# A long convolution by Fourier transform: 128 x 32 with 64x64 tiles becomes 256 x 16 with 32x32 tiles, under a new order

## The chip, the cores and the metric

The kernel runs on one core of a Trainium2 chip. The core has engines that work side by side, each through its own list of instructions in order: TensorE for matrix products (PE in the profile, with its weight loads shown apart as PEld), VectorE (DVE), ScalarE (ACT), GpSimd (POOL) and SyncE (SP). POOL and SP do little but start DMA transfers here. Matrix products land in PSUM, which has eight banks of 128 partitions by 512 float32 numbers; from there an engine must copy ("evict") them to SBUF, the working memory. The metric is the device time of one execution in microseconds (us), lower is better.

## What is computed

Two independent heads work on 2048 positions of 1024 channels, and their outputs stand side by side in the result.

```python
# head A: short convolution, product, long convolution, gate
k_shift = sum(k_pad[:, t:t + S, :] * shift_k[:, ks - 1 - t] for t in range(ks))   # ks = 4
kv = k_shift * v
y = irfft(rfft(pad(kv)) * rfft(pad(ssm_k)))[:S]          # causal, length 2048 of 4096, per channel
a = q * (y + kv * ssm_D)

# head B: a diagonal complex state space model
Lam_bar = exp(dt * Lam);  B_bar = ((Lam_bar - 1) / Lam)[:, None] * (B_re + 1j * B_im)
h[t] = Lam_bar * h[t - 1] + B_bar @ x[t]                 # 1024 states, 2048 steps
b = 2 * real((C_re + 1j * C_im) @ h[t]) + x[t] * Dskip
```

## The kernel before

**Head B** goes in 16 chunks of 128 positions. For chunk i, 8 tasks `U` (16 matmuls of 128 columns each, L444) make the input projection; `ue` evicts it (ACT); `r1`, `r2`, two scans `sc`, `r3`, `r4` on DVE (L459 to L478) turn it into the states, one after the other from chunk to chunk; eight tasks `y.i.dh.part` (L518, L521), each of four 512-column matmuls and one of 128 columns, make the output products; `ye` evicts and `yst` stores. For chunks 6 to 12 the output products are instead written as `yt` (L499) in 64x64 tiles: the array is used as four small ones, and each matmul has 64 rows and 64 columns of weights. Their skip products are then `yk` (L484). `yf` or a drain guards the first accumulation.

**Head A** is a Fourier transform of 4096 points in three steps, by matrix products with constant matrices. Positions are split as 16 residues `s` by 128.

- *First stage.* `kvm`, `kva`, `kvb`, `kvc` (DVE) make kv for one residue; `am` (L573) multiplies it with F1, two matmuls per half of the channels; `ae` (ACT) evicts, `ast` (POOL) writes it to Ys_kv in DRAM. The filter is transposed (`hT`, `hc`), multiplied by the same matrix (`hm`, L611), evicted (`he`) and written to Ys_h (`hst`). F1 holds zeros in every other row of each of its two halves, one half per parity.
- *Middle stage.* It works on 16 pairs i. `lw` loads the pair's constants into one of three weight slots (`wslot`), `lh` and `lk` load 256 rows of Ys_h and Ys_kv. `sh` and `sk` (L640) transform the filter and kv, `she` and `ske` evict. `sw` copies the filter's real and imaginary rows crosswise by DMA, `pr` (DVE, L666) multiplies, `sa` (L678) transforms back, `sae` evicts, `vst` writes to Vs in DRAM. One `sh`, `sk` or `sa` does half a pair: 4, 4 and 8 matmuls of 64x64 weights by 512 columns, into two PSUM banks.
- *Last stage.* `vl` reads Vs, `a3` (L706) multiplies by G, `a3e` evicts, `qm` gates by q (`qp` loads it), `ost` stores.

All of Ys_h must be in DRAM before the first `lh` can load, all of Ys_kv before the first `lk`, all of Vs before the first `vl`.

**The order** is written out by hand as one long string, `ORDER`. Each word is a task; it issues its instructions at once, so each engine's list, the DMA lists of SP and POOL included, is the string's order cut down to that engine. Behind a colon stand the places that the task uses: `a` for places in one big SBUF arena, `p` for the PSUM banks, `w` for weight slots, `h` for the three state buffers. Nothing else sets priorities: an engine that waits for one task holds up all that follow on it.

Of the kernel before, what the change touches and what calls it, by code (L numbers as in the profile page):

```python
# [21 lines left out]
N1, N2, NFFT = 128, 32, 4096  # L22
NG = 32
NPAIR = NG // 2
NUNITS = 53
NGS = 3
NWS = 3
# [5 lines left out]
def a_constants():  # L33
    g = np.arange(NG)[:, None, None]; l = np.arange(2)[None, :, None]; cc = np.arange(2)[None, None, :]
    k1 = (2 * g + l + 0 * cc).reshape(-1); cs = (cc + 0 * g + 0 * l).reshape(-1)
    m = np.arange(128)
    ang = 2 * np.pi * (m // 2)[:, None] * (k1 + 0.5)[None, :] / N1
    tr = np.where(cs[None, :] == 0, np.cos(ang), -np.sin(ang))
    F1 = np.stack([tr * (m % 2 == p)[:, None] for p in range(2)], axis=1)
    G = np.stack([tr.T * (m % 2 == p)[None, :] * 2 / NFFT for p in range(2)], axis=1)  # L40
    n2 = np.arange(N2); k2 = np.arange(N2)
    W = np.zeros((2, 64, NG, WC))
    for g in range(NG):
        for l in range(2):
            kk = (2 * g + l) + N1 * k2
            phi = 2 * np.pi * np.outer(n2, kk + 0.5) / NFFT
            cph, sph = np.cos(phi), np.sin(phi)
            fw = np.zeros((2, N2, 2, N2))
            fw[0, :, 0, :] = cph
            fw[1, :, 0, :] = sph  # L50
            fw[0, :, 1, :] = -sph
            fw[1, :, 1, :] = cph
# [11 lines left out]
    return f(F1), f(G), f(W)
# [5 lines left out]
wb.3:p4 par_rest tabA2 wbe.3 gz bT.1.1:p5 kp.-1 x.1:a29 U.1.0.0:a30p6 wbe.5 kp.0 wbe.7 kvm.1:a32 kva.1 bT.1.0:p7 kvb.1:a28 bc.1.1 bc.1.0 bl.6.0:a36  # L70
bl.7.1:a37 bl.3.1:a38 bl.7.0:a39 bT.6.1:p0 bc.6.1 bT.6.0:p4 bT.7.1:p1 bc.6.0 bc.7.1 kp.1 kvm.3:a40 kvm.2:a44 kva.3 U.1.0.1 bT.7.0:p3 bT.3.1:p5 bc.7.0
sin1 bc.3.1 U.1.3.0:p7 U.1.3.1 sin2 eo x.0:a48 ue.1.0 U.0.0.0:a50p0 U.0.0.1 U.0.3.0:p4 U.0.3.1 bl.4.1:a49 bc.2.0 ue.0.3 bT.4.1:p1 bc.4.1 ue.0.0 kp.-2
kvm.0:a0 x.2:a52 U.2.0.0:a8p3 kvb.3:a49 U.2.0.1 U.2.3.0:p5 U.2.3.1 ue.2.3 kva.0 bl.3.0:a10 x.5:a11 bl.2.1:a36 bT.2.1:p6 bc.2.1 U.5.0.0:a38p2
U.5.3.0:p4 bl.5.1:a37 bT.5.1:p1 bc.5.1 U.5.3.1 ue.5.3 stt cx.5.0 bl.4.0:a32 z1 bT.3.0:p0 bT.4.0:p5 x.3:a33 kp.2 bc.3.0 bl.5.0:a34 U.1.1.0:p6 kvb.0:a35
U.0.1.0:p1 kvm.4:a40 kva.2 bc.4.0 kva.4 cx.6.1 vp.0:a36 kvc.1 cl.1.1:a10 kvb.4:a32 bT.5.0:p4 cl.2.0:a0 bc.5.0 kvb.2:a1 U.0.1.1 ue.0.1 U.0.2.0:p0
U.0.2.1 ue.1.3 cl.3.1:a2 cl.2.1:a3 cx.7.0 ue.0.2 r1.0:a40 kvc.0 ue.2.0 r2.0:h0 kvm.5:a44 rt sc.0.0 lw.3:w0 sc.0.1 U.1.2.0:p5 U.1.1.1 ue.1.1 U.1.2.1
cl.1.0:a34 ue.1.2 U.5.0.1 ue.5.0 z2 r1.1:a40 r3.0:a20 cT.3.1:p4 U.5.1.0:p1 U.5.1.1 cT.2.0:p7 dd r2.1:h1 ue.5.1 U.3.0.0:a50p0 cx.5.1 cx.6.0 U.3.2.0:p3
U.3.3.0:p6 cl.3.0:a2 cT.1.1:p5 r4.0 U.3.3.1 cc.1.1 ue.3.3 kva.5 cc.3.1 U.3.2.1 cT.2.1:p2 cc.2.1 ue.3.2 U.2.2.0:p1 U.3.0.1 cT.1.0:p5 cc.1.0 cl.0.1:a0
cT.0.1:p6 cc.0.1 am.0.0:p4p2 ae.0.1.0:a36 ue.3.0 ae.0.0.0 U.2.1.0:p3 U.2.1.1 ue.2.1 cT.3.0:p5 cc.2.0 cy.1 am.0.1:p6p2 sc.1.1 ae.0.0.1 ae.0.1.1 sc.1.0
cx.4.0 cl.0.0:a10 U.2.2.1 ue.2.2 r1.2:a24 r3.1:a40 am.1.0:p0p4 r4.1 cx.7.1 U.5.2.0:p3 am.1.1:p7p6 vp.1:a30 cx.4.1 U.5.2.1 ue.5.2 kvc.2 cc.3.0  # L80
# [87 lines left out]
def full_kernel(ctx, tc, A_q, A_k, A_v, A_shift_k, A_ssm_k, A_ssm_D, B_x, B_Lre, B_Lim, B_Bre, B_Bim,  # L168
# [613 lines left out]
```

## Time and profile before

| | |
|---|---|
| median of 3 runs | 358.2 us (356.83 to 359.08) |
| profiled execution | 357.8 us, span 356.1 us |
| granted TensorE clock, mean | 0.995 of full speed |
| instructions in the span | 10361 |
| DMA | 104.10 MB, mean 292 GB/s |
| evictions of the middle stage on ACT | 3 groups of 64, about 0.65 us each |
| wslot loads | 16 of 160 KB, median 3.8 us to landing |

The span runs from the first to the last instruction that the profile shows. A busy time is the union of the instructions' durations on one engine; matmuls overlap, so a group's mean duration is longer than the time between two starts. "Idle before" names what ended the wait ahead of an instruction. L12 is line 12 of the kernel.

### The profile page before, as it was taken

What the parts mean: (1) busy time and instruction counts of PE and PEld (TensorE: products, weight loads), DVE (VectorE), ACT (ScalarE), POOL (GpSimd) and SP (SyncE); (2) the same over time, 40 slices, a digit from 0 to 9 for tenths busy, and PEclk for the clock granted to TensorE, in tenths of its full rate; (3) what the DMA queues carried; (4) which work ended last, traced back from release to release, by engine and by line L of the source; (5) the groups of instructions that cost most, each with busy time, mean ns of one, the idle gap of its engine ahead of it and who ended that gap; (6) DMA issues with size and microseconds to landing.
All of it is one profiled execution on the core that took longest, in us unless ns stands there. A gap on an engine that the chain in (4) does not pass through costs nothing.

```text
span 356.1 us, 10361 instructions
## 1 busy us (share of the span) xinstructions
PE 333.2 (94%) x4378; PEld 232.8 (65%) x4393; DVE 314.1 (88%) x239; ACT 285.4 (80%) x547; POOL 87.5 (25%) x142
## 2 busy tenths in 40 slices
PE   5999999999999999999979999898989998999991
PEld 2889998465947669766835667464766875944440
DVE  4899999999999999999987997987498769997970
ACT  5899998257799989999578998888989996546550
POOL 5000000021515333436140205121421422300250
PEclk9999999999999999999999999999999999999997
DMA  6999987598999999999989999989889998899973
GB/s 212 319 262 299 234 135 202 195 298 190 297 224 353 317 326 296 276 299 322 323 278 337 327 328 352 307 298 324 312 321 308 349 345 290 330 317 389 371 284 148
DMA packets 62826, 104.10 MB, mean 292 GB/s; under 512 B 29582, under 2 KB 31646, under 8 KB 62780
## 3 DMA queue, kind: packets, MB, share of 16 engines
q1 hardware_dynamic: 50012, 59.78, 59.0%
q0 software_dynamic: 12768, 43.67, 33.6%
q8 instruction: 34, 0.56, 0.7%
q14 instruction: 12, 0.10, 0.1%
HBM read 53.62 MB, written 35.13 MB: 249 GB/s over the span
## 4 chain that ended last, share of the span: by engine, by line
PE 63%; DMA 13%; ACT 10%; issue 6%; DVE 4%; POOL 2%; SPq 1%; POOLq 0%; DVEq 0%; ACTq 0%
PE bank L444 24%; PE bank L518 13%; PE bank L499 6%; DMA wslot<-a_c_W 4%; DMA arena<-arena 4%; PE bank L573 4%; PE bank L611 4%; DMA arena<-Xs 3%; ACT BT L414 3%; PE bank L678 2%; PE bank L595 2%; PE bank L640 2%; DVE gslot L472 2%; PE bank L398 2%; DMA arena<-in_B_B_re_dram 2%
## 5 line engine op out<-in xcount | busy, mean ns | idle before, releaser
L444 PEld LDWEIGHTS <-BT 128*128 128x128 bf16 x2048 | 117.9, 98 | 11.2 <-issue 4.3
L444 PE MATMUL bank<-arena,BT 128*128 128x128 bf16 x2048 | 123.8, 220 | 1.5 <-ACT BT L414 0.8
L472 DVE TENSOR_TENSOR_SCAN gslot<-rtab,gslot 128x1040 bf16<-128x1040 f32 x32 | 72.7, 2310 | 3.9 <-ACT gslot L468 3.5
L518 PE MATMUL bank<-CT,gslot 128*128 128x512 bf16 x275 | 68.7, 379 | 0.7
L499 PE MATMUL bank<-CT,gslot 64*64 64x512 bf16 x896 | 56.3, 376 | 0.4 <-DVE gslot L478 0.4
L666 DVE TENSOR_TENSOR arena<-arena 128x4096 bf16<-128x4096 bf16 x16 | 36.6, 2290 | 17.4 <-ACT arena L656 7.6
L446 ACT CAST arena<-bank 128x512 bf16<-128x512 f32 x64 | 39.0, 641 | 10.1 <-PE bank L444 9.8
L518 PEld LDWEIGHTS <-gslot 128*128 128x128 bf16 x288 | 26.3, 98 | 27.4
L499 PEld LDWEIGHTS <-gslot 64*64 64x64 bf16 x896 | 28.6, 107 | 20.6 <-DVE gslot L478 0.9
L656 ACT CAST arena<-bank 128x512 bf16<-128x512 f32 x64 | 36.2, 658 | 5.6 <-PE bank L640 4.7
L649 ACT CAST arena<-bank 128x512 bf16<-128x512 f32 x64 | 35.0, 637 | 4.7 <-issue 1.5
L617 ACT CAST arena<-bank 128x512 bf16<-128x512 f32 x64 | 35.2, 672 | 4.1 <-PE bank L611 2.9
L686 ACT CAST arena<-bank 128x512 bf16<-128x512 f32 x64 | 35.5, 660 | 3.2 <-PE bank L678 3.0
L579 ACT CAST arena<-bank 128x512 bf16<-128x512 f32 x64 | 35.7, 629 | 2.9 <-PE bank L573 2.9
L459 DVE TENSOR_TENSOR arena<-gslot,Z 128x4096 bf16<-128x4096 bf16 x16 | 36.6, 2289 | 0.7
L459 DVE TENSOR_TENSOR arena<-arena,Z 128x4096 bf16<-128x4096 bf16 x16 | 36.5, 2282 | 0.7 <-ACT arena L446 0.6
L660 POOL DMA_DIRECT2D arena<-arena x32 | 17.4, 547 | 70.6 <-ACT arena L649 60.9
L620 POOL DMA_DIRECT2D Ys_h<-arena x32 | 23.3, 730 | 35.8 <-ACT arena L617 35.8
L640 PE MATMUL bank<-arena,wslot 64*64 64x512 bf16 x256 | 23.7, 382 | 6.8 <-DMA wslot<-a_c_W 4.1
L553 DVE TENSOR_TENSOR arena<-arena 128x4096 bf16<-128x4096 bf16 (+3 forms) x16 | 30.0, 1880 | 0.0
L527 ACT CAST arena<-bank 128x512 bf16<-128x512 f32 x32 | 19.8, 645 | 11.4 <-PE bank L521 9.9
L582 POOL DMA_DIRECT2D Ys_kv<-arena x16 | 11.1, 695 | 64.1 <-ACT arena L579 64.0
(101 smaller groups left out, 421.1 us busy)
## 6 DMA issues: line engine op xcount, KB each, us to landing
Ys_kv<-arena POOLq DMA_DIRECT2D x16, 512.0 KB, 6.5
Ys_h<-arena POOLq DMA_DIRECT2D x32, 256.0 KB, 4.7
arena<-Ys_h SPq DMA_DIRECT2D x16, 512.0 KB, 5.4
arena<-arena POOLq DMA_DIRECT2D x32, 256.0 KB, 4.6
arena<-Ys_kv SPq DMA_DIRECT2D x16, 512.0 KB, 7.7
Vs<-arena POOLq DMA_DIRECT2D x16, 512.0 KB, 6.5
arena<-Vs SPq DMA_DIRECT2D x16, 512.0 KB, 6.7
arena<-in_A_k_dram SPq DMA_DIRECT2D x8, 512.0 KB, 5.4
```

What stands on the lines that cost most here:

```text
L444: nc.tensor.matmul(pu[:, w, jl, :], BT[:, 2 * jp + jl, w, d, :], xT[:, d, :], start=(d == 0), stop=(d == ND - 1))
L446: E["ue"] = lambda i, jp: nc.scalar.copy(st["u", i][:, :, 2 * jp:2 * jp + 2, :], st.pop(("pu", i, jp)))
L459: nc.vector.tensor_mul(m, s_, win(Z))
L472: nc.vector.tensor_tensor_scan(gf, rtab[:].rearrange("p j t -> p (j t)"), gf, 0.0, ALU.mult, ALU.add)
L499: mm = nc.tensor.matmul(st["py", i, dh][64 * c:64 * c + 64, :], h[rows, w, j, 2 + 64 * c:66 + 64 * c], CT[rows, j, w, dh * 512:(dh + 1) * ...
L518: nc.tensor.matmul(py, h[:, w, j, 2:GW], CT[:, j, w, dh * 512:(dh + 1) * 512], start=(j == 0 and w == 0), stop=False)
L579: return nc.scalar.copy(st["ysb", n2][:, p, dh * 512:(dh + 1) * 512], st.pop(("pa", n2, p, dh)))
L617: return nc.scalar.copy(st["yh", hf, s][:, p, e, :], st.pop(("pb", hf, s, e, p)))
L649: return nc.scalar.copy(st["hab", i][:, 0, a, l, :], st.pop(("ps", "h", g, l)))
L656: return nc.scalar.copy(st["x16", i][:, a, l, :], st.pop(("ps", "k", g, l)))
L666: nc.vector.tensor_mul(hab, st.pop(("x16", i)).rearrange("p a l d -> p (a l d)").unsqueeze(1).to_broadcast([P, 2, 2 * D]), hab)
L686: return nc.scalar.copy(st["vsb", i][:, a, dh * 512:(dh + 1) * 512], st.pop(("pv", g, dh)))
```

## The change

The transform is factored 256 x 16 instead of 128 x 32. F1 becomes one full matrix of 128 rows by 256 outputs, used as two halves, and G likewise; the number and shape of the first-stage and last-stage matmuls stay. Rows of Ys_kv, Ys_h and Vs are numbered (half, row, residue) instead of (row, half, residue).

The middle stage has weights of 32x32 in place of 64x64. One `sh`, `sk` or `sa` now does a whole pair, with 16, 16 and 32 matmuls of 32x32 weights by 512 columns, which go to four row groups and four column groups of the array, into four banks. A pair's constants take 320 columns instead of 640, so `lw` loads 80 KB. Evictions, crosswise copies, the product `pr` and the stores keep number and size.

`yt`, `yk` and `yf` are used no more: all output products are `y` on the whole array. The last product with q and its store are made in halves for two residues (`qh`, `oh`). `ORDER` is new throughout, all places included; of it the diff shows the beginning and the lines around the first `sh`.

```diff
-N1, N2, NFFT = 128, 32, 4096
-NG = 32
-NPAIR = NG // 2
+N1, N2, NFFT = 256, 16, 4096
+NPAIR = 16
...
+    a = np.arange(128)
+    kc = np.arange(256)
+    ang = 2 * np.pi * a[:, None] * (kc // 2 + 0.5)[None, :] / N1
+    tr = np.where(kc[None, :] % 2 == 0, np.cos(ang), -np.sin(ang)).reshape(128, 2, 128)
+    G = tr.transpose(2, 1, 0) * 2 / NFFT
...
-    wslots = [const.tile([P, 2 * WC], BF16, name="wslot%d" % s) for s in range(NWS)]
+    wslots = [const.tile([P, WC], BF16, name="wslot%d" % s) for s in range(NWS)]
...
-    Yk_w = Ys_kv.rearrange("(k p s) d -> s k p d", p=2, s=16)
+    Yk_w = Ys_kv.rearrange("(p k s) d -> s k p d", p=2, s=16)
...
-    def s2(nm, g):
-        i, a = divmod(g, 2)
-        for l in range(2):
-            st["ps", nm, g, l] = bank()
-        for dh in range(2):
-            for l in range(2):
-                rows = slice(64 * l, 64 * l + 64)
-                nc.tensor.matmul(st["ps", nm, g, l][64 * dh:64 * dh + 64, :], st["w", i][rows, a * WC:a * WC + 64],
-                                 st[nm, i][rows, a, dh * 512:(dh + 1) * 512], start=True, stop=True)
+    def s2(nm, i):
+        for r in range(4):
+            st["ps", nm, i, r] = bank()
+        for g in range(2):
+            for dh in range(2):
+                o = 32 * (2 * g + dh)
+                for r in range(4):
+                    rows = slice(32 * r, 32 * r + 32)
+                    nc.tensor.matmul(st["ps", nm, i, r][o:o + 32, :], st["w", i][rows, 32 * g:32 * g + 32],
+                                     st[nm, i][rows, g, dh * 512:(dh + 1) * 512], start=True, stop=True)
...
+    def sa(i):
+        for b in range(4):
+            st["pv", i, b] = bank()
         for t in range(2):
-            for l in range(2):
-                for dh in range(2):
-                    rows = slice(64 * dh, 64 * dh + 64)
-                    c0 = a * WC + 64 + 128 * l + 64 * t
-                    nc.tensor.matmul(st["pv", g, dh][64 * l:64 * l + 64, :], st["w", i][rows, c0:c0 + 64],
-                                     st["hab", i][rows, t, a, l, :], start=(t == 0), stop=(t == 1))
+            for r in range(4):
+                c0 = 64 + 32 * (4 * t + r)
+                for b in range(4):
+                    rows = slice(32 * b, 32 * b + 32)
+                    nc.tensor.matmul(st["pv", i, b][32 * r:32 * r + 32, :], st["w", i][rows, c0:c0 + 32],
+                                     st["hab", i][rows, t, r, :], start=(t == 0), stop=(t == 1))
...
+    def qh(n2):
+        ot, qt = (st[nm, n2 // 2][:, n2 % 2, :] for nm in ("ot", "qt"))
+        nc.vector.tensor_mul(ot, ot, qt)
+    E["oh"] = lambda n2: spd(oar[:, n2, :], st["ot", n2 // 2][:, n2 % 2, :])
...
-ld_par ld_w:a0 wb.0:p0 par_T:p1 p32 wb.4:p2 wbc:a4 bl.6.1:a52 wbe.0 wb.7:p3 exp1 dve2 wbe.4 wb.6:p4 wbe.6 exp2 wb.1:p5 wbe.1 bl.1.1:a8 dve3 bl.0.1:a9
-bT.0.1:p6 bc.0.1 wb.2:p7 wbe.2 sm_pre sin0 bl.0.0:a10 bT.0.0:p0 bc.0.0 bl.1.0:a11 ld_F wb.5:p1 kring:a12 tabA1:a20a22a24a26 bl.2.0:a28 bT.2.0:p2
...
-hst.1.1.1 hst.1.5.0 hst.1.2.1 hst.1.6.1 hst.1.2.0 hst.1.5.1 hst.1.7.1 hst.1.7.0 lh.1:a26 sh.2:p1p0 she.2.0:a0 she.2.1 sh.3:p7p5 she.3.0 ast.12
-yt.6.0.2 yt.6.0.3 she.3.1 lh.0:a30 sh.0:p3p4 she.0.1:a20 she.0.0 yk.7.0:p1 yk.7.1:p0 sh.1:p7p5 yf.6.she.0.1 yt.6.1.0 ast.15 she.1.0 she.1.1 ast.14
-ast.13 lh.3:a48 sh.6:p4p3 she.6.0:a4 yt.6.1.1 she.6.1 sh.7:p7p5 lh.2:a40 yt.6.1.2 she.7.1 lk.1:a10 sk.3:p4p3 she.7.0 ske.3.0:a48 yt.6.1.3 sk.2:p5p7
...
+bT.0.0:p2 sm_pre wb.3:p1 bl.7.0:a16 tabA1:a18a20a22a24 exp2 wbe.5 wbe.0 bl.6.1:a17 sin0 par_rest wbe.6 bc.0.0 wbe.2 wbe.3 bT.7.0:p6 kp.0 kp.-2 tabA2
+kp.1 kp.-1 kvm.1:a28 kvm.3:a32 kvm.0:a36 kva.3 kvm.2:a40 kvb.3:a52 kva.2 kva.1 bT.6.1:p7 bc.6.1 bc.7.0 bl.0.1:a26 kva.0 kvb.2:a27 kvb.0:a16 kvb.1:a17
...
+sc.8.0 sc.8.1 hst.1.4.0 r3.8:a24 hst.1.4.1 hst.1.0.1 y.6.0.2 y.6.0.3 r4.8 hst.1.3.0 y.7.0.0:p3 hst.1.5.1 qp.5:a36 xl.14:a12 hst.1.2.0 hst.1.5.0
+hst.1.2.1 xs.15 hst.1.3.1 hst.1.1.0 hst.1.1.1 xl.12:a13 hst.1.6.1 ue.9.1 xl.10:a14 hst.1.6.0 lh.1:a42 sh.1:p2p0p6p5 she.1.1:a4 she.1.0 she.1.2 y.7.0.1
+she.1.3 lh.3:a50 sh.3:p7p1p0p2 she.3.1:a32 y.7.0.2 y.7.0.3 she.3.2 she.3.0 y.7.1.0:p6 y.7.1.1 y.7.1.2 she.3.3 ast.11 lh.0:a2 sh.0:p5p1p0p7 she.0.0:a16
+she.0.1 she.0.2 she.0.3 y.7.1.3 ast.13 ye.7.1:a15 y.8.1.0:p2 ast.10 y.8.1.1 ast.14 ast.15 ast.12 sw.1.0 lh.2:a10 ye.7.0 lk.1:a44 ye.6.0 sk.1:p5p1p0p7
```

More of the change, by code (lines that the diff above doesn't have):

```diff
@@ L33, in a_constants @@
 def a_constants():
[L34 to L40, printed above, removed]
@@ L63, in a_constants @@
     f = lambda a: np.ascontiguousarray(a.reshape(128, -1), dtype=np.float32).astype(ml_dtypes.bfloat16)
[L64 removed]
+    return f(tr), f(G), f(W)
 ORDER = """
[L68 to L70 removed]
@@ L71 @@
[L71 to L78, printed above, removed]
@@ L165 @@
+ost.6 y.15.1.1 y.15.0.3 y.15.1.2 oh.14 y.15.1.3 a3e.3.1 a3e.3.0 qm.1 ye.15.0:a13 ye.15.1 ost.1 yst.15
 """
@@ L211, in full_kernel @@
     W3v = W3d.ap().rearrange("p (i m) -> p i m", i=NPAIR)
-    Ys_kv = tc.dram_tile([NG * P, D], BF16, name="Ys_kv")
-    Ys_h = tc.dram_tile([NG * P, D], BF16, name="Ys_h")
-    Vs = tc.dram_tile([NG * P, D], BF16, name="Vs")
+    Ys_kv = tc.dram_tile([NFFT, D], BF16, name="Ys_kv")
+    Ys_h = tc.dram_tile([NFFT, D], BF16, name="Ys_h")
+    Vs = tc.dram_tile([NFFT, D], BF16, name="Vs")
     Xs = [tc.dram_tile([P, D], BF16, name="Xs%d" % i) for i in range(NCH)]
```

252 lines of the change are left out of this document (125 added, 127 removed).

## The prediction

> **What bounds the kernel now.** I first read the page's busy times, then the busy time of each engine by stage. Stage A runs to the first middle matmul (L640) at 175.3 us, stage B to the last one (L678) at 302.9, stage C to the end. The columns are stage, length, then busy time and instruction count of PE, PEld, DVE, ACT and POOL.
>
> ```profile
> PE 333.2 (94%) x4378; PEld 232.8 (65%) x4393; DVE 314.1 (88%) x239; ACT 285.4 (80%) x547; POOL 87.5 (25%) x142
> 175.30:302.90 127.60, 118.68 (x2065) 78.90 (x2066) 106.53 (x54) 112.09 (x228) 31.87 (x53) 1.00 0.92 322
> 302.90:356.10 53.20, 45.29 (x348) 25.80 (x344) 38.96 (x24) 25.10 (x51) 10.35 (x16) 0.97 0.84 306
> 14.20:175.30 161.10, 159.67 (x1918) 122.26 (x1928) 160.05 (x133) 138.26 (x255) 40.25 (x59) 1.00 0.98 269
> ```
>
> In A, PE and DVE are both full from 14.2 us on. In C, PE alone is full until its last matmul. In B, PE, ACT and DVE are all over 80% and none is full.
>
> Busy PE is not PE at work, since matmuls overlap; so I take slots from start to start, out of the order of time (start, length).
>
> ```profile
> 171.80 3.74 PE L444 MATMUL bank<-arena,BT 128*128 128x128 bf16 x64
> 175.46 1.91 PE L499 MATMUL bank<-CT,gslot 64*64 64x512 bf16 x29
> ...
> 224.97 0.39 PE L640 MATMUL bank<-arena,wslot 64*64 64x512 bf16 x4
> 225.19 1.03 PE L499 MATMUL bank<-CT,gslot 64*64 64x512 bf16 x16
> 226.05 0.39 PE L640 MATMUL bank<-arena,wslot 64*64 64x512 bf16 x4
> ...
> 225.84 0.12 PEld L640 LDWEIGHTS <-wslot 64*64 64x64 bf16 x4
> ...
> 302.28 1.03 PE L499 MATMUL bank<-CT,gslot 64*64 64x512 bf16 x16
> 303.25 0.95 PE L444 MATMUL bank<-arena,BT 128*128 128x128 bf16 x14
> ```
>
> Sixteen 64x64 matmuls take 0.86 us (225.19 to 226.05): four share the array, and a group of four costs 0.216, as much as one full matmul of 512 columns. Inside a group the starts lie close together: four weight loads of 107 ns fill 0.12 us, so some 4 ns apart. A full matmul of 128 columns costs 0.056. Entering the tiled form costs 0.09 (64 at 0.056 are 3.58; the next starts after 3.66), leaving it 0.10 (four groups are 0.86; the next starts after 0.97). So 0.195 for a visit.
>
> With these slots I add up the orders. B holds 38 U (34.0), 53 yt (45.8), 12 yk (2.7), 128 middle groups (27.6) and 15 visits (2.9): 113.1 of 127.6 us. PE loses 14.5 there, mostly to waits:
>
> ```profile
> PE bank L640 <- DMA wslot<-a_c_W: 4.1, 4, 1.7
> PE bank L640 <- DMA arena<-Ys_kv: 2.7, 2, 2.3
> PE bank L678 <- DVE arena L666: 1.1, 1, 1.1
> ```
>
> C has 45.7 us of PE work and ends its matmuls 45.7 us after it began; a tail of 7.4 follows (last eviction and store).
>
> **The change, part by part.**
>
> *Middle stage.* 512 matmuls of 64x64 in 128 groups become 1024 of 32x32 in 64 groups of sixteen. No row shows a 32x32 group. If sixteen run side by side, it costs 0.216 and the stage 13.8 instead of 27.6; if only four do, 0.86 and 55.3. I take 0.216: the 64x64 rows show full overlap with different data in each column half, and sixteen starts at 3.5 ns are 0.056, well inside 0.216. The low bound below that is excluded, as 512 columns pass in any case.
>
> *Output products.* yt (64x64 tiles) goes; every y runs on the whole array. A chunk costs the same: 32 slots of 0.216 against 128 quarter slots. But before, yt lay next to the middle tasks in one tiled form. Now each middle task stands between whole-array work: reading the new order gives 44 visits, not 15. A visit costs 0.195 plus the wider spread of sixteen starts (0.042): 0.237, so 10.4 us instead of 2.9.
>
> Over the whole kernel PE goes from 323.5 + 2.9 to 309.6 + 10.4: 6.4 us less, not 13.8.
>
> [...] In this trace loads for the same rows run under matmuls (PEld L499 is loading from 224.98 us, under L640) and the period stays 0.216. [...]
>
> *New order, stage A.* Before the first `sh`, the new order has 57 y instead of 48 y, 2 yt and 2 yk: PE +6.1. DVE has more. The last output product ahead of `sh.1` is y.7.0.0, which waits for r4.7; before it was yt.6, waiting for r4.6:
>
> ```profile
> 173.26 1.22 DVE L478 TENSOR_TENSOR gslot<-arena 128x2048 bf16<-128x2048 bf16 x1
> ```
>
> That is r4.6, done at 174.5, just ahead of the first tiled matmul. All kv work lies ahead of it in both orders, so r4.7 comes one chunk later: r1, r2, two scans, r3, r4 at mean 2.29, 1.22, 2.31, 2.31, 2.29, 1.22, less some 0.08 overlap each, 11.2 us. DVE is full, so nothing hides it: r4.7 at 185.7, and after one y part (0.92) the first `sh` at 186.6. PE's own sum would allow 3 us earlier, which also covers four k loads (2 MB) that SP now issues ahead of most B loads. Should they hold up kvm.1 beyond 14.2 us, every microsecond is lost whole.
>
> *Stage B.* 40 U (35.8), 44 y (40.5), 64 groups (13.8), 44 visits (10.4): 100.5. Of the 14.5 lost I keep 11.8. The wait for Ys_kv (2.7) goes: between first `sh` and first `sk` PE has nine y parts (8.3) and three groups, against 5 yt and six groups before. The wslot waits stay: loads halve to 80 KB, but most reloads have 3.0 to 3.3 us of PE work over them where 3.3 to 3.9 stood. A 160 KB load took 3.8 to land, 64 KB 3.0, so the half load saves 0.6 or so, and the cover is 0.5 thinner. B takes 112.3, to 298.9.
>
> *Stage C.* 45.8 of PE work; behind the last `sa` stand 8 U and 11 y (17.3) for the V round trip, which took 12.9 before (302.9 to the first V landed at 315.8). With the tail, 53.2: the span is 352.1.
>
> *At nothing:* F1t, Gt and stage-three matmuls keep number and shape; Ys and Vs rows are renumbered with pieces of the same size; evictions stay 64 each; the two halves qh cost DVE 0.15 more at the end, where it idles.
>
> **Sum.** 352.1 + 1.7 (execution 357.8 against its span of 356.1) = 353.8. The median, 358.2, is 0.4 over that execution. I say 354.
>
> **Rivals.**
>
> *Evictions set stage B.* ACT's evictions follow each other at 0.48:
>
> ```profile
> 225.40 0.58 ACT L656 CAST arena<-bank 128x512 bf16<-128x512 f32 x1
> 225.89 0.59 ACT L686 CAST arena<-bank 128x512 bf16<-128x512 f32 x1
> 226.36 1.58 ACT L656 CAST arena<-bank 128x512 bf16<-128x512 f32 x3
> ```
>
> B keeps 188 middle evictions, 20 ue and 11 ye: 219 x 0.477 = 104.5, now above PE's 100.5. If ACT is kept as full as PE was (113.1 of 127.6, 89%), B takes 118 and the time is 186.6 + 118 + 53.2 + 1.7 = 359.5. For it: ACT is 88% busy in B now. Against: its in-order queue idled mostly for PE. [...]
>
> *Four banks at once (slower).* A middle task held two banks and now holds four of eight; its first four matmuls touch all of them. Freeing four takes 4 x 0.477 = 1.9 us, and PE, in order, stops with everything behind it when one is late. 48 tasks times a wait w: from w = 0.17 us on it is slower by over 1%; at 0.4, 373. For it: y parts hold one or two banks for several parts. Against: none of PE's waits listed in B is for ACT, so banks have come free in time so far.
>
> *Sixteen tiles do not overlap.* At four side by side, 41.5 us more on PE in B: about 395. Against it stand the 64x64 rows.
>
> **How the numbers follow.** My forecast has a chance of 0.47 (346.5 to 357: the low end is ACT's floor of 104.5 in B; 0.41 of it faster by over 1%, 0.06 within). Evictions: 0.27 (356 to 363; 0.24 within, 0.03 slower). Banks: 0.20 (0.02 within, 0.18 slower). No overlap: 0.06, slower. One per cent, about what a measurement of this kernel can tell from no change, is 354.6 to 361.8. Faster 0.41, same 0.32, slower 0.27. The range, 346.5 to 368, leaves out the no-overlap case and the worse half of the bank case.
>
> **What would show it.** Right: sixteen 32x32 starts within 0.06 us and the next group after 0.216; 44 visits at 0.24; first `sh` near 186.6; B near 112 and C near 53. Wrong: `sh` waiting on ACT for banks; ACT full through B; groups longer than 0.3; or a first `sh` that is earlier because DVE ran ahead.

## The result, and the profile after

The changed kernel takes 370.4 us (median; 369.2 to 370.8) where the kernel before, beside it on the same chip, takes 357.9: a ratio of 1.034, 95% interval 1.030 to 1.039. It is slower, and above the top of the forecast range. Some executions of every kernel are disturbed and take 1 to 3% longer; the ratios here and below leave them out, the medians do not.

From the page of the changed kernel, the row of the granted clock in 40 slices of 9.2 us:

```profile
PEclk9999999999999999999996999998999999999997
```

Busy time of each engine by stage (start and end, length, busy time and instruction count of PE, PEld, DVE, ACT, POOL, then granted clock, DMA share, GB/s), first of the kernel before, then of the changed kernel:

```profile
0.00:177.22 177.22, 171.10 (x2008) 129.11 (x2022) 170.43 (x164) 149.13 (x271) 45.23 (x73) 1.00 0.97 268
177.22:302.07 124.85, 115.93 (x2018) 77.40 (x2013) 103.88 (x53) 110.79 (x225) 31.87 (x53) 1.00 0.92 320
302.07:356.05 53.98, 46.12 (x364) 26.26 (x360) 39.79 (x24) 25.51 (x51) 10.35 (x16) 0.97 0.84 308
```

```profile
0.00:192.47 192.47, 177.16 (x2009) 131.86 (x2023) 183.83 (x172) 150.37 (x273) 46.80 (x75) 1.00 0.91 249
192.47:315.33 122.86, 107.73 (x1870) 66.49 (x1884) 88.76 (x45) 109.08 (x224) 30.56 (x51) 0.96 0.89 317
315.33:369.00 53.67, 45.89 (x354) 25.46 (x327) 39.75 (x25) 25.45 (x51) 9.85 (x15) 0.96 0.81 298
```

Stage A ends 15 us later than before, B is hardly shorter although PE has less to do in it, C is what it was. PE is no longer at full clock in two slices of the middle, which is new.

One slip of the prediction has to be named first. The 175.3 us at which it began stage B are the first *tiled* matmul, a `yt`; the first `sh` of the kernel before starts at 177.22. From the first `sh` to the start of the last `sa`, B was 124.9 us before. Measured so, from the profiled executions (one of each kernel):

| us | before | forecast | after | after against forecast |
|---|---|---|---|---|
| first `sh` | 177.2 | 186.6 | 192.5 | +5.9 |
| B | 124.9 | 112.3 | 122.9 | +10.6 |
| C | 54.0 | 53.2 | 53.7 | +0.5 |
| span | 356.1 | 352.1 | 369.0 | +16.9 |

**Where A's 5.9 us are.** What the forecast took to set the first `sh`, DVE's last step for chunk 7, came within 1 us of the 185.7 that it gave. The changed kernel's order of time on DVE:

```profile
185.24 1.22 DVE L472 TENSOR_TENSOR gslot<-arena 128x2048 bf16<-128x2048 bf16 x1
```

It ends at 186.5. But nothing waited for it: PE got to the product that needs it, y.7.0.0, only at 189.1, and then waited for the filter's rows. The same kernel on PE:

```profile
189.10 1.03 PE L512 MATMUL bank<-CT,gslot 128*128 128x512 bf16 x4
...
192.47 0.44 PE L635 MATMUL bank<-arena,wslot 32*32 32x512 bf16 x16 [2.29 <-DMA arena<-Ys_h]
192.85 1.16 PE L512 MATMUL bank<-CT,gslot 128*128 128x512 bf16 x4
...
195.93 0.66 PE L635 MATMUL bank<-arena,wslot 32*32 32x512 bf16 x16 [1.82 <-DMA arena<-Ys_h]
```

So the first `sh` came when PE's own list and its waits let it. Up to it PE is busy 177.2 us and idle 15.3; before, it was busy 171.1 and idle 6.1. That is 6.1 us more work, as forecast, and 9.2 more of waiting: 2.3 for the filter's rows at the end, 5.6 for B's matrices at the start, 1.3 in between. The waits of PE in the first 40 us, first the changed kernel's, then the kernel before's (in all, times, longest):

```profile
PE bank L392 <- DMA arena<-in_B_B_im_dram: 6.8, 1, 6.8
```

```profile
PE bank L398 <- DMA arena<-in_B_B_im_dram: 0.8, 1, 0.8
...
PE bank L398 <- DMA arena<-in_B_B_re_dram: 0.4, 1, 0.4
```

And the filter's rows went through DRAM more slowly. The DMA issues of the page, changed kernel and kernel before (KB each, median us to landing):

```profile
Ys_h<-arena POOLq DMA_DIRECT2D x32, 256.0 KB, 7.7
```

```profile
Ys_h<-arena POOLq DMA_DIRECT2D x32, 256.0 KB, 4.7
```

The last `he` ends at 175.5, the last `hst` has landed when `lh.1` is issued at 186.4, and `sh.1` can start on what it loads at 192.5; before, `he` ended at 161.5 and the first `lh` was issued at 168.4, 9 us ahead of the first `sh`.

**Where B's 10.6 us are.** By the slots of the forecast (0.056 and 0.216 from start to start, plus the visits) PE's work in B is 100.2 us where 100.5 were forecast, so it loses 22.7 us where 11.8 were kept; before, by the same count, it lost 12.0. The trace lacks 14 records of 512-column matmuls there (1870 of PE against 1884 weight loads), so the work is counted by the weight loads. PE is idle for 15.1 of the 22.7 us (before: 8.9), and some 4 us more go to a clock at half speed (last section): these two are nearly all that came on top. Waits of the changed kernel from 192.4 to 315.8 us:

```profile
DVE arena L659 <- ACT arena L649: 14.1, 2, 11.0
...
DVE arena L659 <- DMA arena<-arena: 12.1, 4, 7.1
...
PE bank L670 <- DVE arena L659: 7.3, 6, 2.8
...
PE bank L635 <- DMA arena<-Ys_h: 4.1, 2, 2.3
...
PE bank L635 <- DMA wslot<-a_c_W: 1.9, 3, 0.9
...
PE bank L635 <- DMA arena<-Ys_kv: 0.9, 1, 0.9
```

`sa` (L670) now waits 7.3 us for the product `pr` (L659) where it waited 1.1, and `pr` waits for the crosswise copies and for kv. The first `pr` and the last:

```profile
L659 DVE TENSOR_TENSOR arena<-arena x16: 2266/2286/2294, 210.7 to 312.7; 128x4096 bf16<-128x4096 bf16 x16
```

The product came every 7.29 us before and comes every 6.80 us now: 15 x 0.49 = 7.3 us gained. But from the first `sh` to the first `pr` pass 18.2 us instead of 11.5, because `lk.1` can be issued only at 198.4, behind the last kv store, and `sk.1` runs 8 us later: 6.7 of the 7.3 are given back.

### The profile page after: what moved, and what is told of

Its sections match the earlier page's. It is cut to its first block, busy times and chain, and to the rows that moved or that the text cites. A ratio compares the mean times of both kernels' runs of the same rounds, so it can differ in the third digit from the quotient of the medians.

```text
span 369.0 us, 10027 instructions
## 1 busy us (share of the span) xinstructions
PE 330.8 (90%) x4201; PEld 223.8 (61%) x4233; DVE 312.3 (85%) x240; ACT 284.9 (77%) x547; POOL 87.2 (24%) x141
## 5 line engine op out<-in xcount | busy, mean ns | idle before, releaser
L438 PE MATMUL bank<-arena,BT 128*128 128x128 bf16 x2048 | 126.2, 221 | 1.7 <-ACT arena L677 1.0
L438 PEld LDWEIGHTS <-BT 128*128 128x128 bf16 x2048 | 119.3, 99 | 13.4 <-issue 6.8
L512 PE MATMUL bank<-CT,gslot 128*128 128x512 bf16 x483 | 123.0, 384 | 2.5 <-issue 1.3
L512 PEld LDWEIGHTS <-gslot 128*128 128x128 bf16 x512 | 45.3, 99 | 52.0 <-issue 8.8
L659 DVE TENSOR_TENSOR arena<-arena 128x4096 bf16<-128x4096 bf16 x16 | 36.4, 2286 | 28.3 <-ACT arena L649 14.1
L643 ACT CAST arena<-bank 128x512 bf16<-128x512 f32 x64 | 34.0, 666 | 12.6 <-PE bank L635 12.1
L611 ACT CAST arena<-bank 128x512 bf16<-128x512 f32 x64 | 34.6, 656 | 10.8 <-PE bank L605 8.1
L515 PE MATMUL bank<-Dd,arena 128*128 128x128 bf16 x128 | 28.3, 221 | 0.0
L680 POOL DMA_DIRECT2D Vs<-arena x16 | 11.9, 741 | 47.1 <-ACT arena L677 35.6
L392 PE MATMUL bank<-ident,arena 128*128 128x128 bf16 x192 | 15.9, 242 | 7.1 <-DMA arena<-in_B_B_im_dram 6.8
```

The lines of the kernel that those rows point to most:

```text
L438: nc.tensor.matmul(pu[:, w, jl, :], BT[:, 2 * jp + jl, w, d, :], xT[:, d, :], start=(d == 0), stop=(d == ND - 1))
L512: nc.tensor.matmul(py, h[:, w, j, 2:GW], CT[:, j, w, dh * 512:(dh + 1) * 512], start=(j == 0 and w == 0), stop=False)
L611: return nc.scalar.copy(st["yh", hf, s][:, p, e, :], st.pop(("pb", hf, s, e, p)))
L643: nc.scalar.copy(st["hab", i][:, 0, r, :], st.pop(("ps", "h", i, r)))
L659: nc.vector.tensor_mul(hab, st.pop(("x16", i)).rearrange("p r d -> p (r d)").unsqueeze(1).to_broadcast([P, 2, 2 * D]), hab)
```

## The experiments

Medians in us, with the ratio to the kernel before and its 95% interval. "B" is from the first middle matmul to the start of the last, in the one profiled execution of each kernel. PE's work in B is a sum of slots: matmuls, counted by their weight loads, times 0.056 us (128 columns) or 0.216 us (512 columns; a group of four 64x64 or sixteen 32x32 tiles counts as one), plus 0.195 for each visit to 64x64 tiles and 0.24 to 32x32 tiles. The DMA engines' busy time is their share times B, good to half a us or so. Waits are the idle times of the views; the expectations, quoted as they stood before each run, count them from start to start, which comes out some tenths higher.

### Which half of the change costs time: the order or the tiles

The new order with the 64x64 tiles, weights and DRAM rows of the kernel before; each `sh`, `sk` and `sa` does both halves of its pair, in four banks.

```diff
-N1, N2, NFFT = 256, 16, 4096
-NPAIR = 16
+N1, N2, NFFT = 128, 32, 4096
+NG = 32
+NPAIR = NG // 2
...
+    E["sh"] = lambda i: [s2("h", g) for g in (2 * i, 2 * i + 1)]
+    E["sk"] = lambda i: [s2("k", g) for g in (2 * i, 2 * i + 1)]
...
+    E["sa"] = lambda i: [sa(g) for g in (2 * i, 2 * i + 1)]
```

> The new order with the old transform: 128 x 32, middle stage in 64x64 tiles, each sh, sk and sa doing its two halves one behind the other into the same four banks; weight loads of 160 KB again. All else as in the kernel after. PE has 64 more slots of 0.216 us in stage B (13.8 us) and narrower group starts (44 x 0.04 = 1.8 us less). Theory P (PE sets stage B): 370.4 + 12 = 382 us. Rival L (stage B goes by the latency of the chain transform, evict, copy crosswise, multiply, transform back, with three weight slots, and PE has slack in it): 371 to 376 us; then the smaller tiles alone bring 1 to 5 us and the order is what costs.

375.9 us, ratio 1.045 (1.037 to 1.053), as L had it. So the order by itself costs 4.5%, and with the tiles it is 1% less (the intervals just meet), most of which lies in stage A (first `sh` at 196.7 here, at 192.5 with them), where no tile is at work yet: this execution waits 3.3 us there for the filter's input instead of 1.2, and runs at half clock from 141.5 to 148.3. PE's work in B is 112.1 us here and 100.2 with the 32x32 tiles, 12 less, and B is 124.6 here and 122.9 there. Some 4 us of the 12 went to the half clock, of which this B has none; of the rest, too, little is seen in B.

The same from the other side: the kernel before, with its output products on the whole array and nothing else changed.

```diff
-                for r in (1, 0):
-                    dh = r if s == 0 else 1 - r
...
-                        mm = nc.tensor.matmul(st["py", i, dh][64 * c:64 * c + 64, :], h[rows, w, j, 2 + 64 * c:66 + 64 * c],
-                                              CT[rows, j, w, dh * 512:(dh + 1) * 512], start=False,
...
+                nc.tensor.matmul(st["py", i, s], h[:, w, j, 2:GW], CT[:, j, w, s * 512:(s + 1) * 512],
+                                 start=False, stop=(j == NJ - 1 and w == 1))
```

> The kernel before, with the output products of chunks 6 to 12 on the whole array (one bank after the other, each matmul full) instead of 64x64 tiles; order and places untouched, the guards of the tiled accumulation gone. PE's visits to the tiled form go from 15 to 52. By the measured 0.195 us for a visit: 37 x 0.195 = 7.2 us more on PE. Theory V (visits cost what the slots say, and PE is the bound of stage B before): 357.9 + 5 to 7 = 364 us. Rival W (PE's waits in stage B, 14.5 us, take most of it up): 358 to 361 us.

358.4, ratio 0.997 (0.994 to 1.001): W. Stage B of this kernel:

```profile
177.30:303.00 125.70, 120.92 (x1369) 67.44 (x1380) 103.68 (x53) 111.64 (x225) 31.96 (x53) 1.00 0.91 320
```

PE has 7.0 us more work there, all of it visits, and B is 0.8 longer: what PE loses in B fell from 12.0 to 5.8.

### Why stage A ends late

The five first loads of B's matrices ahead of two of the four k loads (of the long lines of the order, the parts that change):

```diff
-bT.7.0:p6 kp.0 kp.-2 tabA2
-kp.1 kp.-1 kvm.1:a28
+bT.7.0:p6 kp.-1 kp.0 bl.0.1:a26 bl.2.1:a44 bl.1.1:a45 bl.6.0:a46 bl.1.0:a47 tabA2
+kp.1 kp.-2 kvm.1:a28
```

> The kernel after, with one edit at the start of the order: two of the four k loads and then five B loads come before the other two k loads, where all four k loads (2 MB) stood ahead of those five. Measured after: 370.4 us; PE waits 7.0 us for B at 9.7 us, first filter transform at 192.5. Theory S (the start-up wait moves the filter's path, and with it the whole of stage A, by as much as PE loses): the wait falls from 7.0 to 2 or less, the first filter transform comes 4 to 6 us earlier, 365 us. Rival D (DVE sets stage A by r4.7, which ended at 186.5, and the wait lay beside it): the first filter transform moves by less than 1.5 us, 369 to 371 us.

369.6, ratio 1.024 (1.015 to 1.034). In the profiled execution, the fastest of the four, the first `sh` comes at 189.5, the span is 363.7, and no wait for Ys_h is left; the times of the four (365.5 to 371.2) reach from one theory to the other. Its waits of PE in the first 60 us show what took the place of the 6.8:

```profile
PE bank L438 <- DMA arena<-in_B_x_dram: 3.4, 1, 3.4
PE bank L392 <- DMA arena<-in_B_B_im_dram: 2.1, 1, 2.1
```

So the first load of x went ahead of those two k loads too (again the parts that change):

```diff
-kp.-1 kp.0 bl.0.1:a26 bl.2.1:a44 bl.1.1:a45 bl.6.0:a46 bl.1.0:a47 tabA2
-bT.1.1:p5 bc.1.1 x.0:a48 bT.1.0:p2
+kp.-1 kp.0 bl.0.1:a26 bl.2.1:a44 bl.1.1:a45 bl.6.0:a46 bl.1.0:a47 x.0:a48 tabA2
+bT.1.1:p5 bc.1.1 bT.1.0:p2
```

> The changed kernel with the five loads of B ahead of most k loads, as in a1, and the first x load moved ahead of the k loads kp.1 and kp.-2 as well. In a1 TensorE still waited 3.5 us for that x load and 2.4 us for the imaginary part of B in stage A. Theory L (the start of stage A is late because the k loads stand ahead of what TensorE needs): these waits shrink to 2 us or less, the first sh comes at 186 to 188.5 us (a1: 189.5, changed kernel: 192.5), the total is 365 to 366.5 us. Rival D (DVE's chain and the round trip of Ys_h set the first sh, and the k loads that now come later hold up DVE instead): the first sh stays at 189 to 191 us, the total at 367 us or more.

368.2, ratio 1.026 (1.015 to 1.037). The first `sh` comes at 188.4, where L put it, but 3.6 us of waits for B's matrices are left and B gives the gain back: the second `sh` waits 2.7 us for Ys_h, and B is 123.7. L is right on the first `sh` and D on the total. DVE is not what sets the first `sh` here either: its r4.7 ends at 184.9, and PE reaches y.7.0.0 at 187.4. With PE early, the filter's way through DRAM is what is late next.

Two runs take that way out. First `lh` loads rows of the same size straight from the filter input, so it waits for no store (the rows are not the filter's transform):

```diff
-    E["lh"] = lambda i: l2("h", Ys_h, i)
+    Hraw = A_ssm_k.rearrange("d (h s) -> (d h) s", h=2)
...
+        spd(st["h", i], Hraw.rearrange("(g r) d -> r g d", r=P)[:, j:j + 2, :])
```

> The kernel after, with the middle stage's filter loads (lh) taken from the input of the filter in DRAM instead of Ys_h: as many bytes and the same shape, but nothing to wait for. The Ys_h writes stay. So the filter's first stage is computed and stored and not used. Theory Y (the round trip of Ys_h through DRAM ends stage A: PE stood 2.5 and 2.1 us at the first two filter transforms and ran on a lower clock for about 8 us after): all three go, stage B begins at 190 at the latest, total 5 to 7 us less, 364 us. Rival K (the round trip of Ys_kv, landed at 198.2, is right behind and sets the same time): total 0 to 2 us less, 368 to 370 us.

368.3, ratio 1.024 (1.017 to 1.031): K. The first `sh` still comes at 192.0, since PE waited 9.0 us for B's matrices here. Then `lk` as well, from v:

```diff
-    E["lh"] = lambda i: l2("h", Ys_h, i)
-    E["lk"] = lambda i: l2("k", Ys_kv, i)
+    raws = {"h": A_ssm_k.rearrange("d (h s) -> (d h) s", h=2), "k": v}
...
+        spd(st[nm, i], raws[nm].rearrange("(g r) d -> r g d", r=P)[:, j:j + 2, :])
```

> The kernel after with both loads of the middle stage (lh and lk) taken from inputs in DRAM, as many bytes and the same shapes, so that neither the filter's nor kv's first stage is waited for; both are still computed and stored. With the filter's wait alone gone, the time fell by 2 us (368.3), and the wait for Ys_kv in stage B was 4.2. Theory K (the two round trips lie one behind the other at the start of stage B): the first product pr comes at 200 or before instead of 208 to 211, total 362 to 364. Rival N (the ramp is absorbed by what follows): total 367 to 369.

368.9, ratio 1.020 (1.010 to 1.029), by the ratio between K and N. The four runs are 364.5, 366.6, 371.2 and 373.7, and the profiled one is the second. B is 119.5: without either round trip 3.4 us shorter than in the changed kernel, still 7 longer than forecast. The first `pr` comes at 208.0, not at 200 or before as K had it.

### What sets stage B

*The three weight slots.* Six slots in the changed kernel, then four slots in the kernel before, so that a pair's constants can be loaded earlier. Six of the new slots take the room of three old ones; in the kernel before, a table moves aside for the fourth. Of the edits to the order, part of one line is shown:

```diff
-NWS = 3
+NWS = 6
...
-sh.5:p0p1p6p5 she.5.1:a44 she.5.0 she.5.3 she.5.2 lh.6:a18 y.9.0.1 ue.11.3 y.9.1.0:p3 r1.10:a32 r2.10:h1 cy.10 lw.6:w1
+sh.5:p0p1p6p5 she.5.1:a44 she.5.0 she.5.3 she.5.2 lh.6:a18 y.9.0.1 ue.11.3 y.9.1.0:p3 r1.10:a32 r2.10:h1 cy.10 lw.6:w0
```

> The kernel after with six weight slots instead of three (they are half as large as before, so the place is there); each load can start three pairs earlier, nothing else changes. Theory R (the ring of three slots paces stage B: PE waits 2.1 us for wslot, and SP stands at a weight load, with the Ys loads queued behind it, until a transform back is done): the waits for wslot and Ys_kv go, stage B shortens by 3 to 6 us, total 364 to 367. Rival Q (only the direct waits go): 1.5 to 2.5 us, total 368 to 369.

370.6, ratio 1.031 (1.023 to 1.039); neither theory. In the profiled execution, the longest of the four (374.6), the wait for the slots is gone, and that for `pr` is 9.8 instead of 7.3.

```diff
-NWS = 3
+NWS = 4
...
-    iot = const.tile([P, T], F32, name="iot")
+    iot = CT[:, 0, 0, 0:2 * T].bitcast(F32)
```

> The kernel before with four weight slots instead of three (a small table moves into a place that is not yet used, to make the room). PE waits 4.7 us for wslot in stage B. Theory R: these waits go and nothing takes their place: 353 to 355 us. Rival B (the whole-array output products took 37 visits more, 7.2 us of PE, without a change in time, so stage B before has something else that ends as late): 357 to 358.5 us.

359.3, ratio 1.000 (0.997 to 1.004): B. PE's wait for the slots falls from 4.1 to 1.7 us, and those for `pr` and the states (`r4`) rise from 1.5 to 4.8. So the slots do not set the time there.

*The crosswise copies.* In the changed kernel they read a constant of the same size, so they wait for no eviction (the product is not the filter's):

```diff
-        dma(st["hab", i][q:P:2, 1, :, :], st["hab", i][1 - q:P:2, 0, :, :])
+        dma(st["hab", i][q:P:2, 1, :, :], CT[0:64, 0, :, :].rearrange("p w (a d) -> p (w a) d", a=2))
```

> The kernel after with the crosswise copies (sw) taken from a constant that lies in SBUF since early on: same number, size and queue, but they no longer wait for the eviction of the filter's transform, and the product pr no longer waits for a fresh copy. The crosswise terms are thus left out of the result. So far stage B took 120.0 to 125.7 us in six kernels whose PE work in it differs by up to 20 us. Theory C (stage B goes by the chain evict, copy, multiply: PE waits 7.9 us for pr in it, pr waits 12.1 us for copies): PE's waits for pr fall to 3 us or less and stage B shortens by 4 to 8 us, total 363 to 366. Rival E (pr waits for the evictions and loads behind the copies just as long): stage B within 2 us, total 368.5 to 371.

378.8, ratio 1.056 (1.048 to 1.063): both theories missed. The wait for `pr` shrank to 2.3 us as meant, but B is 132.6. The copies now go out as early as POOL allows; they land in 7.5 us (median) instead of 5.6 and the loads of kv in 7.2 instead of 6.3, so they seem to stand in each other's way. B has 20.5 us at half clock here instead of 10.2 (mean granted clock 0.92 instead of 0.96), which lengthens it as well. PE's waits of this kernel in B:

```profile
PE bank L635 <- DMA arena<-Ys_kv: 9.6, 3, 5.1
...
PE bank L635 <- DMA wslot<-a_c_W: 5.1, 3, 3.3
```

This says nothing on the copies' own worth, but it was the first sign that transfers compete.

*The evictions.* Those behind `sa` cut from 512 columns to 128, in the changed kernel and in the kernel before (three quarters of what `vst` stores are not written):

```diff
-        nc.scalar.copy(st["vsb", i][:, b // 2, (b % 2) * 512:(b % 2 + 1) * 512], st.pop(("pv", i, b)))
+        nc.scalar.copy(st["vsb", i][:, b // 2, (b % 2) * 512:(b % 2) * 512 + 128], st.pop(("pv", i, b))[:, 0:128])
```

> The kernel after with the last eviction of each middle bank (sae) cut from 512 to 128 columns; the other columns of the back transform are left out, the bytes stored stay. ScalarE's 64 sae fall from 0.48 to about 0.29 us from start to start, 12 us less of its 104.5 in stage B. From the first to the last product pr, the kernel after takes 102 us, 6.8 for a pair (before: 7.3). Theory A (evictions set that pace, 6.5 us of ScalarE for a pair): 6.1 to 6.3 for a pair, total 8 to 10 us less, 361. Rival M (the pace is set by memory transfers or by waits in the order): 6.6 or more for a pair, total 367 to 371.

368.2, ratio 1.017 (1.008 to 1.026). The four runs are 363.8, 365.1, 371.2 and 371.8. The profiled execution is that of 371.2, and its pace of 6.76 us for a pair of spectra is as without the edit (6.80). Whether the two faster runs are the edit's doing could not be told from this run, so the edit was made in the kernel before as well, where PE has the most work:

```diff
-        return nc.scalar.copy(st["vsb", i][:, a, dh * 512:(dh + 1) * 512], st.pop(("pv", g, dh)))
+        return nc.scalar.copy(st["vsb", i][:, a, dh * 512:dh * 512 + 128], st.pop(("pv", g, dh))[:, 0:128])
```

> The kernel before, with the evictions behind the last middle product cut from 512 to 128 columns (only a quarter of their output is written), which takes some 18 us of ScalarE's work out of stage B and no byte of transfer. Theory T: stage B stays at 123 to 126 us, ratio 0.99 to 1.005. Rival E (the evictions on ScalarE, 110 us busy in stage B, set it): stage B 117 us or less, ratio below 0.98.

358.4, ratio 1.003 (0.999 to 1.007): T. Stage B of the kernel before with small evictions:

```profile
177.20:303.14 125.94, 115.38 (x2018) 75.74 (x2013) 102.97 (x52) 93.61 (x225) 31.87 (x53) 1.00 0.91 320
```

ACT has 17 us less to do (93.6 against 110.8) and the stage is 1 us longer.

*The bytes.* `lh` and `lk` load 64 of 128 partitions, half of their bytes, about a fifth of all that moves in B; the other half of the rows is not loaded:

```diff
-        spd(st[nm, i], Ys.rearrange("(g r) d -> r g d", r=P)[:, 2 * i:2 * i + 2, :])
+        spd(st[nm, i][0:64], Ys.rearrange("(g r) d -> r g d", r=P)[0:64, 2 * i:2 * i + 2, :])
```

> The kernel after with each load of the middle stage (lh, lk) cut to the first 64 of its 128 partitions; the other rows are left out, so the transforms work on what lies there. 8 MB of the 37 MB that stage B moves go; the pieces keep their size. Theory M (transfers set the pace: 2.3 MB for a pair at 317 to 350 GB/s are 6.7 to 7.4 us): 5.8 to 6.3 for a pair, total 8 to 14 us less. Theory A (evictions set it): 6.7 to 6.9 for a pair; the waits for Ys_h and Ys_kv shrink by 1 to 2 us, total 368 to 369.

364.9, ratio 1.019 (1.012 to 1.026), between the theories. Stage B with half loads (the changed kernel's is shown above), and its first and last `pr`:

```profile
193.20:309.30 116.10, 107.42 (x1884) 65.31 (x1884) 90.15 (x46) 108.33 (x224) 30.54 (x51) 1.00 0.88 272
```

```profile
L659 DVE TENSOR_TENSOR arena<-arena x16: 2267/2289/2293, 207.4 to 306.7; 128x4096 bf16<-128x4096 bf16 x16
```

The DMA engines are busy 0.88 x 116.1 = 102.2 us instead of 0.89 x 122.9 = 109.3: 7.1 less, and B is 6.8 shorter. The waits for Ys_h and Ys_kv are gone, that for `pr` is 4.4 instead of 7.3, and PE keeps its clock, which is worth some of the 6.8 by itself. Of the 6.8 us, 4.0 lie before the first `pr`, which comes 14.2 us after the first `sh` instead of 18.2; the pace behind it is 6.62 us for a pair instead of 6.80, not the 5.8 to 6.3 of M. The same edit in the kernel before, whose B keeps its clock with and without it:

> The kernel before, with its loads of Ys_h and Ys_kv cut to 64 of 128 partitions (half of their bytes; the other half of the rows is not loaded), nothing else changed. Theory T (in stage B the transfers are what is full: over all kernels so far the stage is as long as the busy share of the DMA engines makes it, 102 to 115 us, plus 10 to 14 us): the DMA engines lose some 7 us of work, stage B falls from 124.9 to 116 to 119 us, the total by 5 to 8 us, to a ratio of 0.978 to 0.986. Rival P (before the change TensorE's own 113 us of work set stage B): stage B 122 to 126 us, ratio 0.99 to 1.00.

355.7, ratio 0.993 (0.989 to 0.998), where P had it. In the profiled execution, the fastest of ten, B falls by 5.0, to 119.9, between T and P; the loss of DMA work was 14 us, twice what T counted:

```profile
177.69:297.59 119.90, 115.66 (x2020) 76.60 (x2016) 103.24 (x53) 110.27 (x225) 31.88 (x53) 1.00 0.84 261
```

Of the 5.0 us, 2.2 lie before the first `pr`, and the pace goes from 7.29 to 7.10. PE works 112.9 of the 119.9 us and is idle for 4.2: with the loads light, PE is the nearest bound there. Then both edits in the changed kernel (the two diffs above together):

> The changed kernel with both: loads of Ys_h and Ys_kv cut to 64 partitions as in a8, and the last evictions cut to 128 columns as in a7. Theory T: as a8, stage B 113 to 116.5 us, ratio to the kernel before 1.01 to 1.02. Rival E (transfers and evictions are both at their limit, so that only cutting both frees the stage): stage B 108 us or less, the ratio 0.995 or below.

360.9, ratio 1.011 (1.003 to 1.019): T.

```profile
191.17:304.27 113.10, 103.48 (x1870) 64.26 (x1884) 91.28 (x47) 91.30 (x224) 31.23 (x52) 0.98 0.90 272
```

Once the loads are light, 17 us of evictions are worth 3.0 us of B in the profiled executions, at a pace of 6.42; the intervals of the two ratios overlap.

Stage B by what the engines had to do in it:

| kernel | B | PE's work | ACT busy | DMA busy |
|---|---|---|---|---|
| before | 124.9 | 112.9 | 110.8 | 114.9 |
| before, products on the whole array | 125.7 | 119.9 | 111.6 | 114.4 |
| before, small evictions | 125.9 | 112.9 | 93.6 | 114.6 |
| before, half loads | 119.9 | 112.9 | 110.3 | 100.7 |
| new order, 64x64 | 124.6 | 112.1 | 109.7 | 114.6 |
| after | 122.9 | 100.2 | 109.1 | 109.3 |
| after, small evictions | 122.2 | 100.2 | 91.1 | 111.2 |
| after, half loads | 116.1 | 100.2 | 108.3 | 102.2 |
| after, both | 113.1 | 100.2 | 91.3 | 101.8 |

With the full loads B lies between 122 and 126 us here whether PE has 100 or 120 us of work and ACT 91 or 112; in the other runs with full loads it was 119.5 at the least (both round trips taken out) and 132.6 at the most (copies from a constant). Half of the load bytes moved it by 5 to 7 us, of which the 15 steps from product to product hold 2.7 to 2.8.

The busy share of the DMA engines does not say that they are full. In the changed kernel a fifth fewer bytes left it at 0.88 instead of 0.89, while the rate fell from 317 to 272 GB/s; and in a stretch of 3.4 us (193.63, last section) they moved 413 GB/s. What does fall with the bytes is the time to landing: the crosswise copies, untouched by the edit, took 4.6 us instead of 5.6, the stores to Vs 4.4 instead of 5.9. Whether the gain comes from free engines or from loads that land sooner, these runs do not tell apart.

### The sum of the causes

The changed kernel with the early loads of B's matrices and x, with `lh` and `lk` straight from the inputs (the values are then not the transforms), and with half of their bytes:

```diff
+        st[nm, i] = sb(2).rearrange("p (g d) -> p g d", g=2)
+        j = 2 * (i % 8)
+        spd(st[nm, i][0:64], raws[nm].rearrange("(g r) d -> r g d", r=P)[0:64, j:j + 2, :])
...
+    E["lh"] = lambda i: lraw("h", i)
+    E["lk"] = lambda i: lraw("k", i)
```

> a9 and, in addition, the 256 rows of each pair are loaded straight from inputs of the same size in place of Ys_h and Ys_kv (so no load waits for its store; the values are not the transforms), and only 64 of their 128 partitions (as in a8). So the late loads at the start, the round trips and half of the load bytes of stage B are taken out together. Theory S (these three hold the whole difference): first sh at 186 to 188.5 us, stage B 112 to 116 us, stage C 53.5 us, total 353 to 359.5 us, no slower than the kernel before. Rival O (something else in the new middle stage is still open, such as the chain from eviction over copies to product): stage B 117 us or more, total 361 us or more.

360.5, ratio 1.000 (0.994 to 1.005) to the kernel before, whose median in these runs was 360.5. First `sh` 188.5, B 115.7, C 53.7; the median is 1.0 us above the top of S. So these three make up for the whole 3.4%. But the bytes are no cause that the change brought: the kernel before moves them too, and with half loads it is faster itself. Against that kernel (spans of 357.9 and 351.9 us, the latter of its fastest run; the ratios are 0.7% apart, not 1.7%) this one has its first `sh` 10.8 us later, B 4.2 shorter, and C 0.6 shorter. The 10.8 lie near the 9.4 us that the forecast had for DVE's chain of one more chunk, but the chain is not what holds the first `sh`: r4.7 ends at 185.6 here, and PE, which waited 3.3 us for B's matrices, reaches y.7.0.0 only at 187.5. And B's 12.6 forecast of gain are 4.2 even with light loads.

## Why the prediction was wrong, step by step

- **"185.7" for r4.7** held as a number (186.5). The path did not: in the changed kernel and in the three runs with early loads, PE came to y.7.0.0 1.3 to 2.6 us after r4.7 had ended, so PE's list with its waits set the first `sh`. That 186.6 came within 2 us of the 188.4 with early loads is in part luck.
- **"PE's own sum would allow 3 us earlier, which also covers four k loads (2 MB)"** failed. The wait for B's matrices alone cost PE 6.8 us at 10 us, where 0.8 + 0.4 stood before: 5.6 us more, which used up the 3 and made PE 2.6 us later than r4.7. The text had looked at what the k loads do to `kvm.1`, not at the B loads behind them on the same queue. Moving five loads and one more brought the first `sh` from 192.5 to 188.4: this term was 4 us.
- **No term for Ys_h.** The forecast priced neither the last `hst` nor `lh.1`. As measured, `he` at 175.5, 4.3 us to the issue of the last store, 6.6 from there to the issue of `lh.1` and 6 for the load make 192.4, later than PE and DVE. It cost 2.3 us at the first `sh` and 1.8 at the second. That the stores took 7.7 us to land instead of 4.7 could not have been read from the page of before; that the last `he` moves late in the order could.
- **The cost of groups and visits** held. Sixteen tiles share the array: in the changed kernel an `sa` of two groups is followed 0.44 us later by an `sh`, which is 2 x 0.216, so the second group of an `sa` exposes no weight load.

```profile
216.62 0.65 PE L670 MATMUL bank<-arena,wslot 32*32 32x512 bf16 x32
217.06 0.56 PE L635 MATMUL bank<-arena,wslot 32*32 32x512 bf16 x16
```

  An `sh` to the next whole-array start takes 0.38 us (192.47 to 192.85): 0.216 and 0.16 for the spread and for leaving, which with 0.09 for entering is the forecast's 0.24 for a visit.
- **"Of the 14.5 lost I keep 11.8 … B takes 112.3"** is the step that failed most: the work held (100.2 against 100.5), but 22.7 us were lost. The step priced B as PE's work and a constant of waits. In its place the runs show that the waits grow when PE's work shrinks: with 12 us less work under one order B fell by 1.7, and with 7.0 us more under the other it rose by 0.8, since PE lost 5.8 us instead of 12.0. The forecast's own row of B had ACT at 88% and the DMA engines at 0.92, and the prediction read past the latter column. After the change these engines are busy for 109.3 us in B, which in 112.3 us would have been a share of 0.97; the kernels with full loads reached 0.87 to 0.92 here.
- **"The wait for Ys_kv (2.7) goes"** failed: 0.9 of it stays at PE, and `pr.1` waits 11.0 us for kv, since `lk.1` can load only at 198.4.
- **Rival "evictions set stage B"** had the right shape, PE's saving buying next to nothing, and its 118 for B came nearer than the forecast's 112.3. But the evictions alone were not the limit here: cut by 17 to 18 us they gave 0.7 us of B in the changed kernel, none in the kernel before, and 3.0 under half loads.
- **Rival "four banks at once"** did not happen: counted from start to start, the middle tasks wait 3.0 us for ACT in B, 0.06 us for each of the 48, where 0.17 was its point; and all of PE's waits for ACT there are 6.4 us, where they were 4.8 before. **"Sixteen tiles do not overlap"** did not happen either.
- **Stage C** held: 53.2 against 53.7.

Together: of A's 15.3 us, 6.1 are more work on PE, which the forecast had, 5.6 the late loads at the start, 2.3 the filter's way through DRAM, and 1.3 other waits; and B, which was to give 12.6 back, gave 2.0. Shown is that the new order carries the loss, that neither PE's work nor the evictions alone move B by more than 2 us, and that half of the load bytes moves it by 5 to 7. Open is what sets the pace from product to product, 6.4 to 7.5 us in all of these kernels: neither lighter evictions nor lighter loads alone brought it down by more than 0.2. Open too is what holds B at 113 us when loads and evictions are both light, with PE at work for 100 of them, and how much of the differences the lowered clock (below) is.

## What to carry to other kernels

Before crediting a saving on one engine, write down for that stage the busy share of every engine and of the DMA engines too: where several stand near 0.9, as here, taking 12 us of work from one was worth under 2 us. Do not carry the waits over as a constant. When an order is rewritten, walk each queue from its first instruction: four loads put ahead of others at 10 us cost 4 us at 190 us, and each store-and-reload through DRAM that ends near the path needs a term of its own, issue to landing twice (6.6 and 6 us for the filter's here).

## What was not expected of the hardware

TensorE lost half its clock (granted 0.50) for 10.2 us in the middle of a dense kernel. The changed kernel's windows around the two places (columns as above):

```profile
190.22:193.63 3.41, 1.16 (x20) 0.57 (x21) 3.32 (x2) 0.63 (x2) 0.00 (x0) 1.00 1.00 346
193.63:197.05 3.42, 1.27 (x20) 0.44 (x19) 3.28 (x3) 1.80 (x4) 1.13 (x2) 0.50 1.03 413
197.05:200.46 3.41, 3.41 (x10) 1.29 (x10) 2.45 (x2) 1.67 (x4) 0.54 (x1) 0.50 0.99 360
...
244.83:248.24 3.41, 0.92 (x49) 0.59 (x50) 3.41 (x2) 1.22 (x4) 0.00 (x0) 1.00 0.72 284
248.24:251.66 3.42, 3.42 (x32) 3.30 (x31) 1.99 (x2) 2.88 (x6) 0.24 (x1) 0.50 0.57 156
```

The granted clock is 0.50 for 6.83 us from 193.63 on, which is 1.2 us after the first wait for Ys_h (2.3 us) had ended and before the second (1.8 us) began, and 0.50 again for 3.41 us from 248.24 on, 1.4 us after a wait of 2.8 us for `pr`; whole-array matmuls of 512 columns start 0.43 us apart in it instead of 0.216. PE is at work for some 8 of these 10.2 us, so they cost it an estimated 4 us. The kernel before had no such piece between 14.5 us, where the record of its clock begins, and 352.4, in its last stage. The first piece is twice as long as the second, and the two falls lie 54.61 us apart, 16 times the 3.413 of the second, as if the clock followed a fixed beat; no more than these two falls speak for it. PE was not idle for all of the 3.41 us ahead of a fall: it was busy for 1.16 and 0.92 of them. The second window at 0.50 comes after one with 1.27 us of work, and full clock after windows that are full of work (3.41 and 3.42). Cut on this beat, every other window of the changed kernel from 197.05 to 316.51 has PE busy for 1.9 us or more, and none of them is followed by a fall. If the waits brought the clock down, which no run shows apart, they cost more here than their own length: an estimated 4 us on top of 2.3 and 2.8.
